# A home of their own for four sums of x, W' of A moved, W' ahead of the denominators, and a new order of TensorE's steps, in a gated mix of two linear-attention blocks

## The chip, the cores and the metric

One core of one Trainium2 chip runs the kernel. The metric is device time in microseconds (us). The kernel before takes 176.55 us, the median of three runs (176.12 to 176.67).

## The reference

Two linear-attention blocks, A and B, work on the same x (2,048 tokens by 640), and a sigmoid gate mixes their outputs. 32 heads have 20 columns each; phi(t) is t + 1 above 0 and exp(t) elsewhere, plus 1e-6.

```python
qkv = (x @ wqkv).reshape(B, S, 3, H, Dh) ...       # q, k, v by head
pq, pk = phi(q), phi(k)
kv = einsum("bhsd,bhse->bhde", pk, v);  z = einsum("bhsd->bhd", pk)
o = einsum("bhqd,bhde->bhqe", pq, kv) / (einsum("bhqd,bhd->bhq", pq, z) + 1e-6)
block = o.reshape(B, S, D) @ wo
out = g * A(x) + (1 - g) * B(x),   g = sigmoid((x * gate_w).sum(-1))
```

## The kernel before

Everything is bf16 with sums in fp32 PSUM (8 banks). The kernel never forms v: it multiplies pk's transpose by x (units G), then by wv (kv), then by wo, which gives one 640 by 640 matrix W' for each block; the output is scaled pq times W' of A plus scaled pq times W' of B. Products of 2 by 2 blocks are made with seven products in place of eight (a Strassen-Winograd scheme), which takes sums and differences of the operands on VectorE beforehand and combining steps on ScalarE and VectorE in between.

The stages, in order of time:

- Keys (0 to 48 us): x times wk for 16 tiles of 128 tokens, with phi on ScalarE and VectorE (L635 and L636 on TensorE).
- G and Q (48 to 106 us): five units G0 to G4 of seven steps, each step eight matmuls of 320 or 321 columns (L1029), woven together with five units Q0 to Q4 of seven steps, each two or three matmuls of 512 columns (L910). Q makes the queries of tokens 0 to 1,023 (blocks 0, 1). A step is named by its product, as in `G2.5` or `Q4.7`; a unit's steps come as 1, 2 and 5, 6, 3, 7, 4, and 6, 3, 7 and 4 add to a PSUM bank after a copy or combine. In G these are copies at L1058, combines at L1063 and sums z at L1077, and in Q copies at L965 and L919, combines at L924, and phi at L940 to L957.
- The middle (103 to 131 us): `kvA`, `kvB` (L1176), the denominators `dA0`, `dB0` (L1282, then VectorE L1304, ScalarE ln and exp, spread DMAs fx on SP, and the scaling of pq at L1349), the bursts of W' `wA0`, `wA1`, `wB0`, `wB1` (L1208, copied out at L1223 or L1225, stored to DRAM and loaded again in another layout by SP), and the queries of tokens 1,024 to 2,047: eight plain steps `R1A` to `R4B` (L997) and one seven-product unit `R0` (L910).
- Output (131 to 172 us): eight pairs of token tiles, O0 to O7, seven steps of five matmuls of 320 columns each (L1418), copies at L1434, L1457, L1462 and L1483, combines at L1441, and stores on SP.

The order of TensorE's steps is written out by hand in the string `MAIN` (L48). A planner in the kernel (`Sched`) takes it as it stands for TensorE, and orders the other engines' work by its own table of costs, due times and priorities; it also gives out PSUM banks. `TURN` is the planner's own charge for a change of the array's shape: full 128 by 128 (mode 0), denominators (1), W' (2), kv (3). `QD` and `RD` name the query tiles whose relu and add run as one VectorE instruction (L955, L1012); the others use ScalarE for the relu (L943, L1014) and VectorE for the add (L957, L1015).

SBUF is full, and buffers share space by age. `PKS` holds pk (columns 0 to 20,479, five units of 4,096) and behind it, from `SSB` = 20,480, the sums of pk, 3,072 columns for each unit. When G unit u has made its last product (`ulast[u]`), its part is free. Into these parts go, later, the sums of x for the seven-product query groups (`XU`, made by `x_sums` at L883: sums 1, 2, 4 at SSB, 5 and 3 elsewhere), the copies `SV`, W' of A (`WP["A"]`) and half of the output tiles (`ot`). Before the change the first group (Q, p = 0) and the second (R0, p = 1) use the same space for sums 1, 2 and 4, so that the second group's sums wait for all of Q's matmuls (`qpe[0]`); they are all made at token `X2` and wait for kvA too.

Of the kernel before, what the change touches and what calls it, by code (L numbers as in the profile page):

```python
# [11 lines left out]
D = 640  # L12
# [32 lines left out]
NPU = 5  # L45
SSB = 20480
RELUB = (3, 5, 7, 9, 11, 13)
MAIN = """G0.1 G1.1 G2.1 G1.2 G3.1 G2.2 G0.2 G1.5 G0.5 G1.6 G0.6 G1.3 G0.3 G2.5 G1.7 G2.6 G0.7 G2.3 G2.7 G0.4  # L48
G1.4 Q1.1 Q0.1 Q1.5 G2.4 Q0.2 Q0.5 Q0.6 G3.2 G3.5 Q0.3 G3.6 Q0.7 Q1.6 Q1.3 G3.3 Q2.5 G3.7 Q1.7 Q2.1
Q1.2 Q0.4 Q2.2 G3.4 Q2.6 Q3.1 Q4.1 Q4.5 Q2.3 Q1.4 Q3.2 Q4.6 Q2.7 G4.1 Q2.4 Q4.2 Q3.5 Q4.3 Q4.7 Q3.6  # L50
G4.2 G4.5 Q3.7 G4.6 Q4.4 Q3.3 Q3.4 G4.7 kvA X2 G4.3 G4.4 dA0 wA0 R1B wA1 LA dB0 S1 S0
kvB R2A wB0 R1A R3B R4A wB1 T1 R4B R0.1 R0.5 R2B R3A R0.2 R0.6 O0.1 O0.5 O3.1 O2.5 R0.7
R0.3 O0.2 O3.2 O2.1 O3.5 R0.4 O0.6 O3.6 O0.3 O3.3 O2.6 O2.2 O3.7 O1.1 dA1 dB1 S2 S3 O0.7 O2.3
O2.7 O1.2 O1.6 O0.4 O1.5 O1.7 O2.4 O4.1 O5.1 O7.1 O3.4 O1.4 O4.2 O5.2 O7.2 O5.5 O6.1 O5.6 O4.5 O6.2
O6.6 O5.7 O4.6 O5.3 O6.5 O7.6 O4.3 O4.7 O7.5 O7.7 O4.4 O7.3 O6.7 O5.4 O1.3 O6.3 O6.4 O7.4"""
RS = (0,)
PB = {}
PQH = (0,)
TP = {1: -0.5, 2: -1, 3: -0.4, 4: -0.3}
WPDVE = ("A1", "B0",)  # L60
QD = ("0.0A0", "0.1A0", "0.1B0", "0.2A0", "0.2B0", "0.3A0", "0.4B0", "0.4B1",)
RD = ("A1", "B0",)
LATE = {"ACT": 110.0, "DVE": 80.0}

# [32 lines left out]

HOP = 60.0  # L100
TURN = 100.0

class Sched:
# [16 lines left out]
    def run(self):  # L121
        todo = {e: [o for o in self.ops if o.eng == e] for e in self.ENGS}
        at = {e: 300.0 for e in self.ENGS}
        bus, mode = [0.0], 0
        live = {}
        left = {}
        for o in self.ops:
            for b in set(o.ins) | set(o.outs):
                if b.pool:
                    left[b] = left.get(b, 0) + 1  # L130

        def can(o, t):

            w = 0.0
            if o.behind is not None and o.behind.start is None:
                return None
            for d in o.deps:
                if d.end is None:
                    return None
                w = max(w, d.end + (0.0 if d.eng == o.eng == "PE" else HOP))  # L140
            skip = set()
            for b in o.outs:
                if b.pool and b.slot is None:
                    got = self.pick(b, max(w, t), skip)
                    if got is None:
                        return None
                    w = max(w, got[0]) if got[0] > t + 1e-6 else w
                    skip |= set(range(got[1], got[1] + b.n))
            return max(w, t) if o.eng == "PE" else w

        n = len(self.ops)
        while len(self.order) < n:
            best = None
            for e in self.ENGS:
                cand = todo[e]
                if not cand:
# [12 lines left out]
            if best is None:  # L169
                raise RuntimeError("stuck: " + ", ".join(c[0].name for c in todo.values() if c))  # L170
            (w, _, _), o, e = best
            for b in o.outs:
                if b.pool and b.slot is None:
                    self.take(b, w)
            for b in o.outs:
                o.deps += b.war
            w = max(w, at[e])
            if e == "PE" and o.mode != mode:
                w, mode = w + TURN, o.mode
            o.start = w  # L180
# [123 lines left out]
def body(nc, A_x, A_wqkv, A_wo, B_x, B_wqkv, B_wo, gate_w, out, log=None):  # L304
# [69 lines left out]
    PQ = {(X, 2 * p + h): PP[X, p][:, :, h, :] for X in XS for p in range(2) for h in range(2)}  # L374
    WVAf = WVA[:, :, :].rearrange("p c f -> p (c f)")
    WP, KVL = {}, {}
    for X, wp, kv in (("A", SSB + 6144, WVAf[:, 1920:2280]), ("B", 16384, PKS[:, 19584:19944])):
        WP[X] = PKS[:, wp : wp + NC * D].rearrange("p (g n) -> p g n", g=NC)
        KVL[X] = kv.rearrange("p (u f) -> p u f", u=NU)
    WST = {}  # L380
    for r, a in enumerate((GSAf[:, 0:1920], WVAf[:, 0:1920])):
        WST["A", r] = a.rearrange("p (u f) -> p u f", u=3)
        WST["B", r] = TXf[:, 1920 * r : 1920 * r + 1920].rearrange("p (u f) -> p u f", u=3)
    OST = {"os": [PKS[:, 8192 + D * k : 8832 + D * k] for k in range(NOS)], "ot": [PKS[:, SSB + D * k : SSB + D * k + D] for k in range(NOT)]}
    ZM = DEN[:, :].rearrange("p (i h) -> p i h", h=32)
    GGX = GSBf[:, 0:1024]
    GTX = EKT[:, 2576:3600]
# [482 lines left out]
    def x_sums(p, after):  # L870
        t1, t2 = 1024 * p, 1024 * p + 512
        a11, a12, a21, a22 = [XT[:, c : c + 2, lo : lo + 512] for lo in (t1, t2) for c in (0, 2)]
        for k, in0, in1, need in (
            (1, a21, a22, ()),
            (2, a11, XU[1], (1,)),
            (5, XT[:, 4, t1 : t1 + 512], XT[:, 4, t2 : t2 + 512], ()),
            (4, a12, XU[2], (2,)),
            (3, a21, a11, (1,)),
        ):
            bxu[p, k] = Buf("xu")  # L880
            op(
                "DVE",
                lambda e, out=XU.get((k, p), XU.get(k, a21)), in0=in0, in1=in1: e.tensor_tensor(out=out, in0=in0, in1=in1, op=ALU.subtract),  # L883
                dve2(512 if k == 5 else 1024),
                ins=[bxu[p, j] for j in need],
                outs=[bxu[p, k]],
                after=after,
                name="xu%d" % k,
            )

# [5 lines left out]
    def qu_unit(p, g):  # L896
# [33 lines left out]
        def post(X, h, pv, ins):  # L930
# [31 lines left out]
        def step(n):  # L962
# [297 lines left out]
    def wp_load(X, halves, lo, hi):  # L1260
# [316 lines left out]
```

## Time and profile before

| | |
|---|---|
| median of three runs | 176.55 us (176.12 to 176.67) |
| the profiled execution | 176.08 us, of which the span is 174.6 |
| TensorE busy | 171.1 us (98%), 1,320 matmuls recorded |
| its weight loads | 108.0 us, 1,335 |
| VectorE busy | 135.6 us (78%), 238 instructions |
| ScalarE busy | 114.2 us (65%), 218 instructions |
| granted TensorE clock | 1.0 |

A line such as L1029 is a line of the kernel; a row names engine, operation, output and inputs, shape and count. PE is TensorE's matmuls, PEld its weight loads, DVE VectorE, ACT ScalarE, SP the queue that issues most DMAs. The end of a matmul is modelled, so that rows of PE overlap; starts are better to go by. A few matmul records are missing in any trace; the weight loads are complete.

### The profile page before, as it was taken

The numbers are of one execution on the slowest core, as the hardware profiler recorded it, in microseconds if no ns is written. First come the engines' busy times: TensorE is split into PE (matmuls) and PEld (weight loads), VectorE is DVE, ScalarE is ACT, GpSimd is POOL, SyncE is SP. The second block draws the span as 40 slices with busy tenths as digits, with TensorE's granted clock in tenths as the row PEclk, the third lists the DMA queues.
The fourth block names the chain that finished last, engine by engine and source line by source line (L and its number), as shares of the span: only waits on it lengthen the run. The fifth ranks groups of instructions, "written<-read, shape, count | busy, mean of one in ns | idle before, by whom it ended". The sixth has DMA issues, their size and how long they took to land.

```text
span 174.6 us, 3344 instructions
## 1 busy us (share of the span) xinstructions
PE 171.1 (98%) x1320; PEld 108.0 (62%) x1335; DVE 135.6 (78%) x238; ACT 114.2 (65%) x218; POOL 5.1 (3%) x16
## 2 busy tenths in 40 slices
PE   9999999999999999999999999999999999999995
PEld 5555555555577767666655666655556667777773
DVE  2275996999999755846868879999999995898342
ACT  5378888988841221648699793867899865566332
POOL 2000000000000520000000000000000000000000
PEclk9999999999999999999999999999999999999999
DMA  6979999980000083554261001467670021450135
GB/s 198 295 142 195 190 374 364 350 158 6 4 0 0 0 71 82 99 130 101 41 184 41 0 4 39 97 187 185 243 188 18 0 75 33 92 192 0 38 122 179
DMA packets 33035, 20.59 MB, mean 118 GB/s; under 512 B 18260, under 2 KB 32892, under 8 KB 33020
## 3 DMA queue, kind: packets, MB, share of 16 engines
q1 hardware_dynamic: 32062, 19.76, 44.3%
q10 hardware_dynamic: 958, 0.63, 1.1%
q8 instruction: 10, 0.16, 0.4%
q14 instruction: 5, 0.04, 0.1%
HBM read 10.88 MB, written 4.26 MB: 87 GB/s over the span
## 4 chain that ended last, share of the span: by engine, by line
PE 90%; DVE 6%; ACT 2%; issue 1%; DVEq 0%
PE ps L1418 22%; PE ps L635 19%; PE ps L1029 19%; PE ps L910 12%; PE ps L997 9%; PE ps L636 6%; PE ps L562 1%; DVE WVA L1223 1%; ACT EQ L940 1%; DVE PKS L883 1%; PE ps L1282 1%; PE ps L1208 1%; PE ps L575 1%; DVE WKW L1063 1%; ACT PQ L943 1%
## 5 line engine op out<-in xcount | busy, mean ns | idle before, releaser
L635 PE MATMUL ps<-WKW,XT 128*128 128x512 bf16 x154 | 43.2, 382 | 0.0
L636 PE MATMUL ps<-WKW,XT 128*128 128x128 bf16 (+1 forms) x160 | 35.2, 220 | 0.3
L635 PEld LDWEIGHTS ps<-WKW,XT 128*128 128x128 bf16 x160 | 15.7, 98 | 19.1 <-DMA WKW<-in_A_wqkv_dram 0.3
L681 ACT ACTIVATE EKT<-ps 128x640 bf16<-128x640 f32 x32 | 22.4, 705 | 6.5 <-PE ps L636 5.8
L1029 PE MATMUL ps<-TX,PKS 128*128 128x321 bf16 (+1 forms) x160 | 23.8, 300 | 0.0
L1029 PEld LDWEIGHTS ps<-TX,PKS 128*128 128x128 bf16 x160 | 15.6, 98 | 7.2 <-DVE DEN L1077 0.3
L1029 PE MATMUL ps<-XN,PKS 128*128 128x321 bf16 (+1 forms) x120 | 17.7, 300 | 0.0
L1058 ACT ACTIVATE EKT<-ps 128x321 f32<-128x321 f32 (+1 forms) x15 | 6.4, 440 | 14.9 <-PE ps L1029 8.8
L636 PEld LDWEIGHTS ps<-WKW,XT 128*128 128x128 bf16 x160 | 15.8, 98 | 0.0
L1029 PEld LDWEIGHTS ps<-XN,PKS 128*128 128x128 bf16 x120 | 11.6, 98 | 5.2
L761 DVE TENSOR_TENSOR PKS<-PKS 128x1280 bf16<-128x1280 bf16 (+2 forms) x20 | 13.1, 686 | 0.1
L684 DVE TENSOR_SCALAR EKT<-EKT 128x1280 bf16<-128x1280 bf16 (+1 forms) x18 | 8.2, 454 | 5.9 <-ACT EKT L681 5.7
L940 ACT ACTIVATE EQ<-ps 128x512 bf16<-128x512 f32 x18 | 11.1, 614 | 2.1 <-DVE ps L924 1.4
L1063 DVE TENSOR_TENSOR WKW<-ps,EKT 128x320 bf16<-128x320 f32 x15 | 7.3, 490 | 6.4 <-PE ps L1029 5.8
L1008 ACT ACTIVATE EQ<-ps 128x1024 bf16<-128x1024 f32 x8 | 8.2, 1024 | 3.3 <-PE ps L997 2.6
L720 DVE SCALAR_TENSOR_TENSOR PKS<-ps,EKT 128x640 bf16<-128x640 f32 x12 | 9.9, 821 | 0.1
L910 PE MATMUL ps<-XT,WQA 128*128 128x512 bf16 x34 | 9.5, 379 | 0.1
L997 PE MATMUL ps<-XT,WQA 128*128 128x512 bf16 x37 | 9.0, 380 | 0.3 <-DVE PKS L1304 0.2
L997 PE MATMUL ps<-XT,WQB 128*128 128x512 bf16 x39 | 9.1, 380 | 0.2 <-issue 0.2
L693 ACT ACTIVATE PKS<-ps 128x640 bf16<-128x640 f32 x12 | 8.4, 698 | 0.0
L953 DVE TENSOR_SCALAR EQ<-EQ 128x512 bf16<-128x512 bf16 (+1 forms) x19 | 6.0, 322 | 2.7 <-ACT EQ L940 2.7
L1441 DVE TENSOR_TENSOR PKS<-ps,PKS 128x320 bf16<-128x320 f32 x8 | 3.9, 490 | 5.2 <-PE ps L1418 5.2
(155 smaller groups left out, 307.3 us busy)
## 6 DMA issues: line engine op xcount, KB each, us to landing
out_dram<-PKS SPq DMA_DIRECT2D x15, 160.0 KB, 1.8
XN<-in_A_x_dram SPq DMA_DIRECT2D x1, 2240.0 KB, 9.3
WKW<-in_A_wqkv_dram SPq DMA_DIRECT2D x5, 160.0 KB, 3.8
WKW<-in_B_wqkv_dram SPq DMA_DIRECT2D x5, 160.0 KB, 3.9
WQA<-in_A_wqkv_dram SPq DMA_DIRECT2D x1, 800.0 KB, 10.9
WQB<-in_B_wqkv_dram SPq DMA_DIRECT2D x1, 800.0 KB, 13.7
WVA<-in_A_wqkv_dram SPq DMA_DIRECT2D x1, 800.0 KB, 12.5
PKS<-in_B_wqkv_dram SPq DMA_DIRECT2D x1, 800.0 KB, 5.0
```

What stands on the lines that cost most here:

```text
L635: e.matmul(a[:, 0:512], l, WK[X][:, c, 0:512], start=(c == 0), stop=(c == NC - 1))
L636: return e.matmul(a[:, 512:w], l, WK[X][:, c, 512:w], start=(c == 0), stop=(c == NC - 1))
L681: op("ACT", lambda e, i=i, ps=ps: e.activation(evg(i), psg(ps), ACT.Exp), act_cost(D), ins=[ps] + first, outs=[ek, b], name="ke")
L693: op("ACT", lambda e, X=X, ps=ps: e.activation(pkt(X, t), psg(ps), ACT.Relu), act_cost(D), ins=[ps], outs=[rk], name="kr")
L720: lambda e, X=X, i=i, ps=ps: e.scalar_tensor_tensor(pkt(X, t), psg(ps), 0.0, evg(i), op0=ALU.max, op1=ALU.add),
L761: lambda e: e.tensor_tensor(out=out, in0=a, in1=b, op=ALU.subtract),
L910: r = e.matmul(PS[:, ps.slot, :], w, x, start=(first and i == 0), stop=(i == len(prs) - 1), skip_group_check=not first)
L940: o = [op("ACT", lambda e: e.activation(EQ[:, eq.slot + h, :], pv(), ACT.Exp), act_cost(512), ins=ins, outs=[eq], name="qe")]
L997: r = e.matmul(PS[:, ps.slot + h, :], WQ[X][:, c, g::5], XT[:, c, 1024 + 512 * h : 1536 + 512 * h], start=(c == 0), stop=(c == NC - 1))
L1029: r = e.matmul(PS[:, ps.slot, 0:w], reg[:, j, :], mov(j, w), start=(first and j == 0), stop=(j == 7), skip_group_check=not first)
L1063: lambda e: e.tensor_tensor(out=GT[:, dst.slot, lo : lo + HC], in0=PS[:, ps.slot, 0:HC], in1=PT[:, src.slot, 0:HC], op=ALU.add),
L1418: r = e.matmul(PS[:, ps.slot, 0:HALF], reg(g), mov(g), start=(first and g == 0), stop=(g == NC - 1), skip_group_check=not first)
```

## The change

1. The second group's sums 1, 2 and 4 of x get 3,072 columns of their own, at SSB + 6,144, the part of G unit 2. They now wait for `ulast[2]`, sum 5 for `ulast[1]`, and only sum 3 for kvA.
2. That space was W' of A's. It moves to SSB - 128, into the part of unit 0 (and the last 128 columns of pk), and its load waits for all of Q's matmuls and the last G unit in place of the fourth. The output tiles `ot` move from SSB to SSB + 3,072.
3. In `MAIN`, `wA0` comes ahead of `dA0`, and `kvB` ahead of `dB0`. The planner charges a turn from mode 1 to mode 2 with 190 instead of 100.
4. `MAIN` is laid out anew: the steps of G, Q, R0 and O stand in another order. The middle's sequence of R steps changes from R1A R3B R4A and R2B R3A at the end to R1A R4A R3B and R3A R2B.
5. `QD` names other tiles (two of the eight differ); `RD` names A0 as well. The plain relu of A (tokens 1,024 and on) waits for the scaling of blocks 0 and 1 only from step 2 on.

```diff
-MAIN = """G0.1 G1.1 G2.1 G1.2 G3.1 G2.2 G0.2 G1.5 G0.5 G1.6 G0.6 G1.3 G0.3 G2.5 G1.7 G2.6 G0.7 G2.3 G2.7 G0.4
-G1.4 Q1.1 Q0.1 Q1.5 G2.4 Q0.2 Q0.5 Q0.6 G3.2 G3.5 Q0.3 G3.6 Q0.7 Q1.6 Q1.3 G3.3 Q2.5 G3.7 Q1.7 Q2.1
-Q1.2 Q0.4 Q2.2 G3.4 Q2.6 Q3.1 Q4.1 Q4.5 Q2.3 Q1.4 Q3.2 Q4.6 Q2.7 G4.1 Q2.4 Q4.2 Q3.5 Q4.3 Q4.7 Q3.6
-G4.2 G4.5 Q3.7 G4.6 Q4.4 Q3.3 Q3.4 G4.7 kvA X2 G4.3 G4.4 dA0 wA0 R1B wA1 LA dB0 S1 S0
-kvB R2A wB0 R1A R3B R4A wB1 T1 R4B R0.1 R0.5 R2B R3A R0.2 R0.6 O0.1 O0.5 O3.1 O2.5 R0.7
...
-O6.6 O5.7 O4.6 O5.3 O6.5 O7.6 O4.3 O4.7 O7.5 O7.7 O4.4 O7.3 O6.7 O5.4 O1.3 O6.3 O6.4 O7.4"""
+MAIN = """G0.1 G1.1 G0.2 G3.1 G1.2 G0.5 G2.1 G0.6 G2.2 G1.5 G1.6 G0.3 G0.7 G1.3 G1.7 G3.5 G0.4 G2.5 G1.4 Q1.1
+G2.6 G3.6 G2.3 G2.7 Q1.5 G3.7 Q1.6 Q0.1 Q1.3 G2.4 Q1.7 Q4.1 Q1.2 G3.2 G3.3 Q0.5 Q0.6 Q0.2 Q2.5 G3.4
+Q0.3 Q1.4 Q0.7 Q2.1 Q4.5 Q0.4 Q3.1 Q4.6 Q4.2 Q2.6 Q2.3 Q4.3 Q2.2 Q4.7 Q3.6 Q3.2 Q4.4 G4.1 Q2.7 Q3.5
+Q3.7 G4.5 G4.2 G4.6 Q3.4 Q2.4 G4.7 Q3.3 kvA X2 G4.3 G4.4 wA0 dA0 R1B wA1 LA kvB dB0 S0
+R2A S1 wB0 R1A R4A R3B wB1 T1 R4B R3A R0.5 R0.1 R2B O0.1 R0.6 O2.5 O0.5 R0.2 R0.7 O3.1
...
+O6.6 O5.5 O4.5 O7.6 O6.7 O5.7 O4.3 O6.4 O5.3 O4.7 O6.3 O7.2 O7.5 O5.4 O7.7 O7.3 O4.4 O7.4"""
-QD = ("0.0A0", "0.1A0", "0.1B0", "0.2A0", "0.2B0", "0.3A0", "0.4B0", "0.4B1",)
-RD = ("A1", "B0",)
+QD = ("0.0A0", "0.1B0", "0.1B1", "0.2A0", "0.2B0", "0.2B1", "0.3A0", "0.4B0",)
+RD = ("A0", "A1", "B0",)
-TURN = 100.0
+TURN, TURNS = 100.0, {(1, 2): 190.0}
-                w, mode = w + TURN, o.mode
+                w, mode = w + TURNS.get((mode, o.mode), TURN), o.mode
-    for X, wp, kv in (("A", SSB + 6144, WVAf[:, 1920:2280]), ("B", 16384, PKS[:, 19584:19944])):
+    for X, wp, kv in (("A", SSB - 128, WVAf[:, 1920:2280]), ("B", 16384, PKS[:, 19584:19944])):
-    ... "ot": [PKS[:, SSB + D * k : SSB + D * k + D] for k in range(NOT)]}
+    ... "ot": [PKS[:, SSB + 3072 + D * k : SSB + 3712 + D * k] for k in range(NOT)]}
+    for k in (1, 2, 4):
+        XU[k, 0] = XU.pop(k)
+    for i, k in enumerate((1, 2, 4)):
+        XU[k, 1] = PKS[:, SSB + 6144 + 1024 * i : SSB + 7168 + 1024 * i].rearrange("p (c s) -> p c s", c=2)
-            after=[ulast[3]] if X == "A" else [],                       # load of W'
+            after=qpe[0] + [ulast[NPU - 1]] if X == "A" else [],
-            x_sums(1, qpe[0] + kva)
+            x_sums(1, lambda k: kva if k == 3 else [ulast[1 if k == 5 else 2]])
```

More of the change, by code (lines that the diff above doesn't have):

```diff
@@ L47 @@
 RELUB = (3, 5, 7, 9, 11, 13)
-MAIN = """G0.1 G1.1 G2.1 G1.2 G3.1 G2.2 G0.2 G1.5 G0.5 G1.6 G0.6 G1.3 G0.3 G2.5 G1.7 G2.6 G0.7 G2.3 G2.7 G0.4
-G1.4 Q1.1 Q0.1 Q1.5 G2.4 Q0.2 Q0.5 Q0.6 G3.2 G3.5 Q0.3 G3.6 Q0.7 Q1.6 Q1.3 G3.3 Q2.5 G3.7 Q1.7 Q2.1
-Q1.2 Q0.4 Q2.2 G3.4 Q2.6 Q3.1 Q4.1 Q4.5 Q2.3 Q1.4 Q3.2 Q4.6 Q2.7 G4.1 Q2.4 Q4.2 Q3.5 Q4.3 Q4.7 Q3.6
-G4.2 G4.5 Q3.7 G4.6 Q4.4 Q3.3 Q3.4 G4.7 kvA X2 G4.3 G4.4 dA0 wA0 R1B wA1 LA dB0 S1 S0
-kvB R2A wB0 R1A R3B R4A wB1 T1 R4B R0.1 R0.5 R2B R3A R0.2 R0.6 O0.1 O0.5 O3.1 O2.5 R0.7
-R0.3 O0.2 O3.2 O2.1 O3.5 R0.4 O0.6 O3.6 O0.3 O3.3 O2.6 O2.2 O3.7 O1.1 dA1 dB1 S2 S3 O0.7 O2.3
-O2.7 O1.2 O1.6 O0.4 O1.5 O1.7 O2.4 O4.1 O5.1 O7.1 O3.4 O1.4 O4.2 O5.2 O7.2 O5.5 O6.1 O5.6 O4.5 O6.2
-O6.6 O5.7 O4.6 O5.3 O6.5 O7.6 O4.3 O4.7 O7.5 O7.7 O4.4 O7.3 O6.7 O5.4 O1.3 O6.3 O6.4 O7.4"""
+MAIN = """G0.1 G1.1 G0.2 G3.1 G1.2 G0.5 G2.1 G0.6 G2.2 G1.5 G1.6 G0.3 G0.7 G1.3 G1.7 G3.5 G0.4 G2.5 G1.4 Q1.1
[3 more added lines that the diff above has]
+R2A S1 wB0 R1A R4A R3B wB1 T1 R4B R3A R0.5 R0.1 R2B O0.1 R0.6 O2.5 O0.5 R0.2 R0.7 O3.1
+R0.3 O0.2 O3.2 O3.5 R0.4 O2.1 O0.6 O0.3 O3.6 O3.3 O2.2 O2.6 O3.7 O1.1 dA1 dB1 S3 S2 O0.7 O1.2
+O2.7 O2.3 O0.4 O1.6 O1.5 O3.4 O1.7 O5.1 O4.1 O6.1 O2.4 O1.3 O1.4 O4.2 O6.2 O7.1 O5.2 O6.5 O5.6 O4.6
+O6.6 O5.5 O4.5 O7.6 O6.7 O5.7 O4.3 O6.4 O5.3 O4.7 O6.3 O7.2 O7.5 O5.4 O7.7 O7.3 O4.4 O7.4"""
 RS = (0,)
@@ L383, in body @@
         WST["B", r] = TXf[:, 1920 * r : 1920 * r + 1920].rearrange("p (u f) -> p u f", u=3)
-    OST = {"os": [PKS[:, 8192 + D * k : 8832 + D * k] for k in range(NOS)], "ot": [PKS[:, SSB + D * k : SSB + D * k + D] for k in range(NOT)]}
+    OST = {"os": [PKS[:, 8192 + D * k : 8832 + D * k] for k in range(NOS)], "ot": [PKS[:, SSB + 3072 + D * k : SSB + 3712 + D * k] for k in range(NOT)]}
     ZM = DEN[:, :].rearrange("p (i h) -> p i h", h=32)
@@ L874, in x_sums @@
             (1, a21, a22, ()),
-            (2, a11, XU[1], (1,)),
+            (2, a11, XU[1, p], (1,)),
             (5, XT[:, 4, t1 : t1 + 512], XT[:, 4, t2 : t2 + 512], ()),
-            (4, a12, XU[2], (2,)),
+            (4, a12, XU[2, p], (2,)),
             (3, a21, a11, (1,)),
@@ L882, in x_sums @@
                 "DVE",
-                lambda e, out=XU.get((k, p), XU.get(k, a21)), in0=in0, in1=in1: e.tensor_tensor(out=out, in0=in0, in1=in1, op=ALU.subtract),
+                lambda e, out=XU.get((k, p), a21), in0=in0, in1=in1: e.tensor_tensor(out=out, in0=in0, in1=in1, op=ALU.subtract),
                 dve2(512 if k == 5 else 1024),
@@ L886, in x_sums @@
                 outs=[bxu[p, k]],
-                after=after,
+                after=after(k),
                 name="xu%d" % k,
@@ L937, in post @@
             bpq[b, NC * XS.index(X) + g] = pqf
-            home = {("B", 0): lambda: [ulast[1]], ("A", 0): lambda: [], ("B", 1): lambda: list(qpe[0]), ("A", 1): lambda: qpe[0] + pqs_op["A", 0] + pqs_op["A", 1] + fx_op[2] + ([ulast[3]] if h else [])}[X, p]()
+            home = {("B", 0): lambda: [ulast[1]], ("A", 0): lambda: [], ("B", 1): lambda: list(qpe[0]), ("A", 1): lambda: qpe[0] + (pqs_op["A", 0] + pqs_op["A", 1] + fx_op[2] if g > 1 else []) + ([ulast[3]] if h else [])}[X, p]()
             one = ["%d.%d%s%d" % (p, g, X, i) in QD for i in range(2)]
@@ L969, in step @@
             elif n == 5:
-                mm(pz, True, [(WU[1][:, c, g::5], XU[1][:, c, :]) for c in range(2)] + [(wq("B", 4), xt(4, 1))], wqs + [bwu[1], bxu[p, 1]])
+                mm(pz, True, [(WU[1][:, c, g::5], XU[1, p][:, c, :]) for c in range(2)] + [(wq("B", 4), xt(4, 1))], wqs + [bwu[1], bxu[p, 1]])
                 d[5] = save(s5, pz)
             elif n == 6:
-                mm(px, False, [(WU[2][:, c, g::5], XU[2][:, c, :]) for c in range(2)], [bwu[2], bxu[p, 2]], [d[1]])
+                mm(px, False, [(WU[2][:, c, g::5], XU[2, p][:, c, :]) for c in range(2)], [bwu[2], bxu[p, 2]], [d[1]])
                 d[2] = save(s2, px)
             elif n == 3:
-                mm(pz, False, [(wq("B", 2 + c), XU[4][:, c, :]) for c in range(2)] + [(wq("B", 4), XU[5, p])], wqs + [bxu[p, 4], bxu[p, 5]], [d[5]])
+                mm(pz, False, [(wq("B", 2 + c), XU[4, p][:, c, :]) for c in range(2)] + [(wq("B", 4), XU[5, p])], wqs + [bxu[p, 4], bxu[p, 5]], [d[5]])
                 comb(pz, s2, False)
@@ L991, in qp_unit @@
         dst = PP[X, 1][:, g, :, :]
-        home = list(qpe[0]) + ([ulast[3]] + pqs_op["A", 0] + pqs_op["A", 1] + fx_op[2] if X == "A" else [])
+        home = list(qpe[0])
+        if X == "A":
+            home += [ulast[3]] + (pqs_op["A", 0] + pqs_op["A", 1] + fx_op[2] if g > 1 else [])
         def fn(e):
@@ L1499, in body @@
                     w_sums([ulast[0]])
-                    x_sums(0, [ulast[0]])
+                    x_sums(0, lambda k: [ulast[0]])
                     qsteps = [qu_unit(0, k) for k in range(NC)]
```

## The prediction

> **What bounds the kernel now.** First the page: busy times, then the span in slices and the chain that ended last.
>
> ```profile
> span 174.6 us, 3344 instructions
> ...
> PE 171.1 (98%) x1320; PEld 108.0 (62%) x1335; DVE 135.6 (78%) x238; ACT 114.2 (65%) x218; POOL 5.1 (3%) x16
> ...
> PE 90%; DVE 6%; ACT 2%; issue 1%; DVEq 0%
> ```
>
> TensorE (PE) is busy from its first matmul to its last, and the chain is TensorE itself. A gain must come from holes in its stream, or not at all. So next the waits, those of the weight loads (PEld), where a TensorE step waits:
>
> ```profile
> PEld ps L1208 <- issue: 1.1, 3, 0.4
> ...
> PEld ps L1418 <- ACT PKS L1462: 0.3, 2, 0.2
> ...
> PEld ps L1029 <- DVE DEN L1077: 0.3, 1, 0.3
> ```
>
> Away from the start and from changes of the array's shape ("issue", and L1208's and L1282's other rows) two name another engine: L1029 on VectorE's z sum (L1077), L1418 on ScalarE's copy (L1462). The timeline around the first:
>
> ```profile
> 61.80 0.26 DVE L1077 SCALAR_TENSOR_TENSOR DEN<-EKT,ps,CST 128x32 bf16<-128x32 f32 x1
> ...
> 62.11 1.48 PEld L1029 LDWEIGHTS ps<-TX,PKS 128*128 128x128 bf16 x12 [0.27 <-DVE DEN L1077]
> ```
>
> This is G2.5, which needs the PSUM bank of G1.3. G1.3, G0.3 and G2.5 signal their ends at 61.09, 62.19 and 63.39 in the trace: 1.09 for G0.3, 1.21 for G2.5, so the wait loses 0.12. It also gives my rule of thumb: the z sum ended at 62.05 and the stream went on at 63.39 - 1.09 = 62.30, so a release must come 0.25 ahead of a step's place. The second (136.42 and 137.10, O2.1 and O3.5) loses 0.02 by the same reckoning. All waits inside the run are worth 0.14.
>
> Then the shape changes, in the timeline from 106 to 113:
>
> ```profile
> 106.81 0.73 PE L1282 MATMUL ps<-PQ,DEN 128*32 128x256 bf16 x20
> ...
> 107.56 0.60 PE L1208 MATMUL ps<-WOA,WVA 64*60 64x320 bf16 x15
> ...
> 110.38 0.60 PE L1208 MATMUL ps<-WOA,WVA 64*60 64x320 bf16 x15
> ...
> 110.92 0.73 PE L1282 MATMUL ps<-PKS,DEN 128*32 128x256 bf16 x20
> ...
> 111.58 1.13 PE L1176 MATMUL ps<-GSB,PKS 128*64 128x60 bf16 x55
> ```
>
> From start to start, denominators (L1282) to W' (L1208) take 0.75, the same 20 matmuls to kv (L1176) 0.66, and W' to denominators 0.54. Only denominators-to-W' is longer, by 0.09.
>
> Last, busy time by stretch (columns: stretch, its length, PE, PEld, DVE, ACT, POOL, clock, DMA, GB/s):
>
> ```profile
> 83.00:104.00 21.00, 20.89 (x147) 12.70 (x147) 16.46 (x40) 18.18 (x38) 0.34 (x2) 1.00 0.21 55
> 104.00:118.00 14.00, 13.62 (x219) 8.57 (x216) 13.87 (x26) 8.81 (x14) 0.00 (x0) 1.00 0.43 105
> ```
>
> ScalarE has little air from 83 to 104, VectorE none from 104 to 118, yet TensorE hardly waits for either. The granted clock is 1.00 throughout.
>
> **The change, part by part.**
>
> *Matmuls.* Both programs hold 1,335 of them, of the same forms; RS is unchanged, and "A0" in RD names a unit that is not built that way. Cost 0.
>
> *Sums of x in their own home.* Three sums of 0.69 (L883) no longer wait for kv of A, nor the 0.42 one; only sum 3 does. Some 2.5 us of VectorE leave the full stretch 104 to 118 for the time after G2.4 and before 83, where VectorE is under two thirds busy (7.39 of 12 us from 71 to 83). Nothing on TensorE waited for them: the first step of the second seven-product group runs at 124.6, the last sum ended at 113.35. Gain 0. They can hurt only by standing in front of a combine (below).
>
> *W' of A in another place.* Its load (SP, 120.44) now waits for the first seven-product group and G4.4 instead of G3.4; both are over before 107 in either order. The second OUT store pool moves with it and still waits for both query groups. Cost 0.
>
> *W' ahead of denominators, kv of B ahead of the second.* Before, the shapes run: full, denominators, W', full, W', denominators, kv, full. After: full, W', denominators, full, W', kv, denominators, full. Seven changes each; the 0.75 one is gone. Denominators to full I price by the later pair, 1.21 for 40 matmuls on the chain at 144.04, so 0.66 for 20: no excess. W' to kv and kv to denominators do not occur; the nearest rows are W' to denominators (0.54, no excess) and kv to full (1.05, the same at both kv). The one excess seen is 0.09, so bounds are -0.09 and +0.09 on top; I take 0, since of the nine kinds in the trace only that one shows an excess of more than 0.03. Term: -0.09, bounds -0.18 to +0.09. The Trainium skill, page "TensorEngine Tiling (Array Packing)", section Tiling Modes (Key Properties), says that changing the tiling mode drains TensorE, whichever mode; counted so, seven against seven gives 0 and the sum below would be 0.09 less of a gain. The rows differ by kind, and no run here yet shows the new kinds.
>
> What moves behind it: the first denominators start 0.54 later. On ScalarE a W' copy (0.97) now stands ahead of ln and exp, on VectorE a 1.15 copy ahead of L1304; then four spread DMAs on SP, in unchanged order (gs, fx, wps, wpl). VectorE reaches L1304 about 0.55 later (108.07 before), and SP's first spread DMA starts no more than that later (109.89); the scaling of PQ that waits for it (114.32 to 126.06) feeds TensorE from O0.1 on, at 131.05. Behind these on the queues stand only such steps. Cost 0; without that cover 0.55. kv of B comes about 0.75 earlier after G4.4. It needs the DMA transpose of the last block:
>
> ```profile
> 106.42 0.49 DVE L1063 TENSOR_TENSOR WKW<-ps,EKT 128x320 bf16<-128x320 f32 x1
> ...
> 106.94 2.52 SPq L429 DMA_TRANSPOSE GSB<-WKW  x2
> ```
>
> The pair landed at 110.83, and kv's loads began at 111.58, so 0.75 of cover would go entirely. But the combine at 106.42 stood behind the first late sum of x (105.72, 0.69), G4.3 having signalled at 105.81; with that sum gone the transposes start up to 0.5 earlier. Cost 0, bound +0.2.
>
> *The new order.* G2.5 no longer follows G0.3: -0.12 (bounds -0.12 and 0). O0.2, O3.2, O3.5 keep their distance: 0.02 stays. New narrow places, each against the 0.25:
> - Q2.5 takes the bank that G3.3's z sum frees, with eight 512-column matmuls (8 x 0.216 = 1.73) between. Chain: release 0.02, a running instruction on VectorE 0.18, combine 0.49, a query combine of 0.69 that stands between, z sum 0.26, less two overlaps of 0.085, plus 0.25: 1.72. Cover 0.01. Such a chain cost 0.12 at G2.5; I take +0.05, bounds 0 and +0.7 (one more 0.69 in front).
> - Q0.4 and Q4.4 follow Q0.7 and Q4.7 by 1.08. Before, Q2.4 followed Q2.7 by 1.09 with the combine ending at 92.99, G4.1's signal at 93.36 and Q2.4's 0.65 later for 3 x 0.216: no loss, 0.12 of cover. Cost 0.
> - Q3.6, Q4.7 and Q3.5 wait at 92 to 96 for copies in a ScalarE run without a gap. At 0.51 from start to start they have 0.04 to 0.1; in the trace such copies (614 mean) start 0.48 to 0.52 apart. Cost 0, bounds 0 and +0.5.
>
> *End.* The last step is O7.4 in both, then a 0.44 copy and a store of 1.6; the stores ahead of it are 0.33 of SP each and 0.6 apart. 0.
>
> **Sum:** -0.09 - 0.12 + 0.05 = -0.16. The profiled execution took 176.08 (span 174.6 and 1.5 around it); the median is 176.55, 0.47 above it. So 176.4 by the median, a profiled one near 175.9. About 0.3%, 0.53 us, is what a measurement of this kernel can tell from no change; this is a third of that.
>
> **Rivals.**
> 1. *ScalarE becomes the bound between 84 and 98 (slower).* For: 18.18 of 21 us busy, and the new order asks for 12 us of it without a pause. Against: the 0.48 spacing. It decides when one further 0.5 instruction stands ahead of a copy at Q3.6, Q4.7 or Q3.5, whose covers are under 0.1: 0.4 each, and as the steps hang on one another, two of them: 0.8 - 0.16 = +0.64, 177.2. Chance 0.11.
> 2. *The home does not pay and nothing else does:* the stalls move (Q2.5 takes the loss of G2.5, a new shape change that of the old). 0: 176.55. Chance 0.25, within the bound.
> 3. *kv of B meets its transposes:* 0.2 lost instead of 0.16 won, 176.6. Chance 0.07, within.
> 4. *Every hole closes:* all of 0.14 and 0.09 with 0.09 more at the new changes, 176.2. Only with the scatter of the runs (176.12 to 176.67) would that show as over 0.3%. Chance 0.12, of which 0.08 beyond the bound.
>
> My forecast, a gain under the bound, holds 0.45. Within 0.3% then is 0.45 + 0.25 + 0.07 + 0.04 = 0.81; faster 0.08; slower 0.11. The range: 176.55 - 0.32 and 0.15 of scatter for the low end, 176.05; at the high end rival 3 with scatter and half of rival 1's price, 176.85.
>
> **What would show it.** Right: no L1077 wait of TensorE near 62; L1208 to L1282 at 0.54 and no step of 0.75; L1176 to L1282 at 1.05; the last matmul 0.1 to 0.2 earlier. Wrong: TensorE waits for L965, L919 or L924 between 81 and 98, a wait of L1176 for a DMA near 110.8, or a last matmul later than before.

## The result, and the profile after

| | before | after |
|---|---|---|
| median of 14 runs each, side by side | 176.34 us (176.02 to 177.02) | 176.90 us (176.43 to 177.64) |
| ratio, 95% interval | | 1.0032 (1.0018 to 1.0046) |
| the profiled execution, its span | 176.08, 174.6 | 176.75, 175.3 |
| end signal of the last key product to end signal of the last product of O7.4 | 124.54 | 125.08 |

The changed kernel is slower by 0.56 us, where 0.16 less was forecast; it lies just above the high end of the range. A second series gave 1.0029 (1.0014 to 1.0044). The last row leaves out the first 48 us, whose input loads scatter by several tenths from run to run: the stretch that the change touches grew by 0.54.

The page of the changed kernel:

```profile
span 175.3 us, 3351 instructions
...
PE 172.2 (98%) x1335; PEld 108.2 (62%) x1335; DVE 135.4 (77%) x236; ACT 114.4 (65%) x218; POOL 4.5 (3%) x16
...
PE 96%; DMA 2%; ACT 0%; issue 0%; DVE 0%
```

The chain that ended last is still TensorE's, but 2% of it is now a DMA, and none was there before. The waits of TensorE name it (matmuls first, then weight loads; the columns are the sum, the number and the longest wait):

```profile
PE ps L1182 <- DMA GSB<-WKW: 0.7, 1, 0.7
...
PEld ps L1182 <- issue: 1.3, 2, 0.9
...
PEld ps L1003 <- DVE EQ L957: 0.2, 1, 0.2
...
PEld ps L1424 <- ACT PKS L1468: 0.2, 1, 0.2
```

L1182 is kv (L1176 before). The wait for the z sum at G2.5 is gone, that for the output copy (L1468) is left. The timeline around kv of B:

```profile
106.17 0.49 DVE L1069 TENSOR_TENSOR WKW<-ps,EKT 128x320 bf16<-128x320 f32 x1
...
106.69 2.52 SPq L433 DMA_TRANSPOSE GSB<-WKW  x2
...
106.86 0.60 PE L1214 MATMUL ps<-WOA,WVA 64*60 64x320 bf16 x15
...
107.40 0.73 PE L1288 MATMUL ps<-PQ,DEN 128*32 128x256 bf16 x20
...
110.34 0.60 PE L1214 MATMUL ps<-WOA,WVA 64*60 64x320 bf16 x15
...
111.59 1.06 PEld L1182 LDWEIGHTS ps<-GSB,PKS 128*64 128x64 bf16 x55 [0.89 <-issue]
111.62 1.13 PE L1182 MATMUL ps<-GSB,PKS 128*64 128x60 bf16 x55 [0.67 <-DMA GSB<-WKW]
...
112.68 0.73 PE L1288 MATMUL ps<-PKS,DEN 128*32 128x256 bf16 x20
```

W' to denominators takes 0.54 (106.86 to 107.40), kv to denominators 1.06: as forecast, no shape change costs more than its matmuls, and the 0.75 of before is gone. But from the first matmul of W' to the first weight load of kv it takes 1.25 (110.34 to 111.59), where the same pair takes 0.53 in a run shown below (e2) in which nothing is late. kv of B stood still for 0.7 us.

It waited for the second of the two DMA transposes issued from 106.69, called gsB4 here (the first is gsB3). gsB3 was issued at 106.69 and landed 2.57 later. gsB4 was issued at 107.94 and landed at 111.48, 3.55 later; in the kernel before, 2.63 later. So the combine and the transposes did start 0.25 earlier (106.17 and 106.69 against 106.42 and 106.94), and the landing was 0.66 later all the same. The DMA view of just these 3.55 us (packets, MB, share of 16 engines; then KB and us from issue to landing):

```profile
q1 hardware_dynamic: 1318, 0.32, 46.0%
q14 instruction: 1, 0.01, 0.5%
...
GSB<-WKW SPq DMA_TRANSPOSE x1, 3.5
```

One packet is not data: 8 KB of instructions for one of the engines, at 109.91, 0.31 us long. In the kernel before the packet of its kind came at 105.74, ahead of both transposes. The same view of gsB4 there, from 108.19 to 110.83, has as many packets of data:

```profile
q1 hardware_dynamic: 1318, 0.32, 61.2%
...
GSB<-WKW SPq DMA_TRANSPOSE x1, 2.6
```

So it was not more data on the DMA engines that made the landing late.

Two measures are used from here on. A step's cover is the time by which what it needs is done ahead of its place in TensorE's order. A step's loss is the distance of its end signal from that of the step before, less what the same matmuls take where nothing is waited for. By it the kernel before loses 0.11 at G2.5 and 0.02 at O3.5, and 0.09 at its denominators-to-W' pair. The changed kernel loses 0.75 at kv of B and 0.02 at O3.5, nothing else. 0.75 - 0.11 - 0.09 = +0.55: the 0.54 of the table, and the 0.56 of the medians.

### The profile page after: what moved, and what is told of

It reads as the page before. It is cut to its first block, busy times and chain, and to the rows that moved or that the text cites. A ratio compares the mean times of both kernels' runs of the same rounds, so it can differ in the third digit from the quotient of the medians.

```text
span 175.3 us, 3351 instructions
## 1 busy us (share of the span) xinstructions
PE 172.2 (98%) x1335; PEld 108.2 (62%) x1335; DVE 135.4 (77%) x236; ACT 114.4 (65%) x218; POOL 4.5 (3%) x16
## 4 chain that ended last, share of the span: by engine, by line
PE 96%; DMA 2%; ACT 0%; issue 0%; DVE 0%
PE ps L1035 22%; PE ps L1424 22%; PE ps L639 20%; PE ps L914 13%; PE ps L1003 9%; PE ps L640 5%; DMA GSB<-WKW 2%; PE ps L566 1%; PE ps L1182 1%; PE ps L1288 1%; PE ps L1214 1%; PE ps L579 1%; ACT PKS L1489 0%; ACT GSA L1231 0%; DVE ONE L465 0%
## 5 line engine op out<-in xcount | busy, mean ns | idle before, releaser
L639 PE MATMUL ps<-WKW,XT 128*128 128x512 bf16 x160 | 44.4, 383 | 0.0
L914 PE MATMUL ps<-XT,WQA 128*128 128x512 bf16 x36 | 10.4, 379 | 0.0
L1003 PE MATMUL ps<-XT,WQA 128*128 128x512 bf16 x40 | 9.2, 381 | 0.0
L923 ACT ACTIVATE PKS<-ps 128x512 f32<-128x512 f32 x12 | 7.4, 624 | 1.6 <-PE ps L914 1.6
```

What stands on the lines that cost most here:

```text
L639: e.matmul(a[:, 0:512], l, WK[X][:, c, 0:512], start=(c == 0), stop=(c == NC - 1))
L914: r = e.matmul(PS[:, ps.slot, :], w, x, start=(first and i == 0), stop=(i == len(prs) - 1), skip_group_check=not first)
L1003: r = e.matmul(PS[:, ps.slot + h, :], WQ[X][:, c, g::5], XT[:, c, 1024 + 512 * h : 1536 + 512 * h], start=(c == 0), stop=(c == NC - 1))
```

## The experiments

The theories, by the letters of the texts below. A: kv of B's cover was moved away, and the transpose landed late because an instruction packet came into it. B: the transpose is late by the place it has in the new order, the packet is chance. C: the position of kv of B costs by itself. A2: behind the wait at kv of B there is a second one at R0.6, and with both gone the forecast 0.16 is there. D and E stand beside it.

The main runs, with the stretch from the last key product to the last product, the 8 KB packet nearest the transposes, gsB4's time from issue to landing, and the losses. A ratio is to the kernel before on the same chip; a dash is a run timed once. The other eight runs, which tried to move the packet, stand under "Packet or place?".

| run | ratio (95%) | stretch | packet at | gsB4 | loss at kv of B | at R0.6 |
|---|---|---|---|---|---|---|
| before | 1 | 124.54 | 105.74 | 2.63 | 0 | 0 |
| changed | 1.0032 (1.0018 to 1.0046) | 125.08 | 109.91, inside | 3.55 | 0.75 | 0 |
| e6, changed again | 1.0029 (1.0014 to 1.0044) | 125.14 | 109.86, inside | 3.62 | 0.82 | 0 |
| e1 | 0.9996 (0.9983 to 1.0008) | 124.72 | 109.64, inside | 3.51 | 0.05 | 0.34 |
| e2 | 1.0012 (0.9997 to 1.0027) | 124.48 | 105.73 | 2.64 | 0.01 | 0.15 |
| e3 | 0.9993 (0.9978 to 1.0009) | 124.59 | 106.37 | 2.64 | 0.06 | 0 |
| e4 | 1.0005 (0.9991 to 1.0018) | 124.60 | 98.48, 105.84 | 2.64 | 0.07 | 0 |
| e5 | 0.9978 (0.9962 to 0.9994) | 124.49 | 110.27, inside | 3.58 | 0.12 | 0 |
| e9 | 0.9987 (0.9968 to 1.0006) | 124.37 | 105.42 | 2.64 | 0.01 | 0 |
| e10 | 0.9983 (0.9968 to 0.9999) | 124.33 | 105.60 | 2.64 | 0.01 | 0 |
| e12 | 1.0024 (1.0011 to 1.0037) | 125.15 | 109.75, inside | 3.59 | 0.79 | 0 |
| e11 | - | 125.03 | 110.04, inside | 3.50 | 0.70 | 0 |

### Is it kv of B, and is it its place? (e1 to e4)

**e1**, the denominators ahead of kv of B again:

```diff
-... R1B wA1 LA kvB dB0 S0
+... R1B wA1 LA dB0 S0 kvB
```

> The changed kernel with one pair exchanged back: the denominators of B stand ahead of kv of B again, as before the change. Theory A (kv of B reaches its place before the last DMA transpose of gs of B has landed, because the denominators no longer stand between, and that transpose takes 3.55 us instead of 2.6): the transpose may land as late as in the changed kernel, but kv of B comes 0.66 to 0.75 later in the order, so it waits 0 to 0.1 instead of 0.75. 176.15 to 176.35 us where the changed kernel has 176.90, and in the trace no loss over 0.1 at kv of B. Rival C (the new order of the whole section costs it, and the wait only shows there): 176.8 to 177.0, with the 0.75 showing at another step. The rival that the later transpose is the new order's traffic says the same as A here.

The transpose landed as late as ever (3.51) and cost 0.05, since the denominators' 0.66 stood in between. kv of B is the place. But the stretch is 124.72, where the forecast 0.16 would give 124.38: 0.34 was lost at a step no one had named, R0.6, of which more below.

**e2**, the changed kernel with VectorE's program made eight instructions longer at its very start:

```diff
+    DUM = sb("DUM", [128, 32], bf)
+    for i in range(8):
+        op("DVE", lambda e, i=i: e.memset(DUM[:, i : i + 1], 0.0), 60.0, name="dum")
```

> The changed kernel with eight small memsets added to VectorE's program at its very start, where it is idle; everything else, the order included, is the same. That shifts VectorE's instruction fetches to some 5 to 7 us earlier work. Theory A with an instruction fetch as the cause (the 8 KB packet at 109.91 us that lies inside the transpose of gsB4): the packet leaves 107.9 to 110.5, the transpose lands 2.6 us after its issue at about 110.55, kv of B waits 0 to 0.05, 176.05 to 176.3 us: about 0.75 below the changed kernel and 0.1 to 0.25 below the kernel before. Rival B (the transpose is late by the new order's own transfers or by its place, and the packet only happens to lie there): the landing stays near 111.4, 176.8 to 177.0. If the packet is another engine's, it stays at 109.9 and so does the time, and nothing is told.

The packet moved to 105.73, so it is VectorE's. With it gone the DMA view of gsB4 and the timeline of the same place read

```profile
q1 hardware_dynamic: 1315, 0.32, 60.9%
...
GSB<-WKW SPq DMA_TRANSPOSE x1, 2.6
```

```profile
110.78 0.60 PE L1217 MATMUL ps<-WOA,WVA 64*60 64x320 bf16 x15
...
111.31 1.03 PEld L1185 LDWEIGHTS ps<-GSB,PKS 128*64 128x64 bf16 x55 [0.18 <-issue]
...
112.37 0.45 PEld L1291 LDWEIGHTS ps<-PKS,DEN 128*32 128x32 bf16 x20
```

(three lines further down in the code). W' to kv takes 0.53. Order, transfers and places are those of the changed kernel, and kv of B lost 0.01. That speaks against B. The time, 1.0012 (0.9997 to 1.0027), is above what was expected, and its interval reaches into that of the changed kernel; the trace is what decides here. Its stretch is 0.6 shorter than the changed kernel's, and only 0.06 below that of the kernel before, since 0.15 was lost at R0.6.

**e3**, the kernel before with kv of B ahead and nothing else of the change:

```diff
-... LA dB0 S1 S0
-kvB R2A wB0 ...
+... LA kvB dB0 S1 S0
+R2A wB0 ...
```

> The kernel before with one pair exchanged: kv of B ahead of the denominators of B and the two selections, as the change puts it, and nothing else of the change. Theory A: the transposes there take 2.57 and 2.63 us and the last lands at about 110.83; kv of B's place is then about 111.0 and its release is needed 0.25 ahead, so it waits 0 to 0.1: 176.2 to 176.45, no different from before. Rival C (the position alone costs, with no late transpose): 0.66 to 0.75 lost, 177.0 to 177.1.

0.9993, 0.06 lost: C falls. Without a late transpose the cover of 0.75 was all spare, but then only just: 0.06 was already missing.

**e4**, e3 with thirty copies on ScalarE to bring its packet into the transpose:

```diff
+    DUM = sb("DUM", [128, 32], bf)
+    for i in range(30):
+        op("ACT", lambda e, i=i: e.activation(DUM[:, i : i + 1], EPSC[:, :], ACT.Copy), 200.0, after=pk_last[-1:], prio=10**7, name="dum")
```

> The run before this one (the kernel before with kv of B ahead of the denominators) with thirty one-column copies added to ScalarE at about 52 to 56 us, where it is idle. That brings ScalarE's instruction fetch, at about 131.8 us in the kernel before, forward to some 109 to 110 us, into the last DMA transpose. Theory A with the fetch as cause: if the 8 KB packet falls between 107.9 and 110.5, the transpose lands 0.5 to 1.0 later, kv of B waits 0.5 to 1.0, 176.8 to 177.3. If the packet falls outside, as without the copies: 176.2 to 176.45. Rival B (a fetch does not matter): 176.2 to 176.45 wherever it falls.

The packet went to 98.5, too far. Nothing is told, but that the copies cost nothing.

### The second hole, R0.6 (e5, e9, e10, e12)

In the middle the change put R3A ahead of R0.5, R0.1 and R2B. e1 shows what that did. ScalarE (ACT, and ACTq for the DMAs that it issues) and the weight loads of R0.6 in e1:

```profile
124.23 1.86 ACTq L433 DMA_DIRECT2D wpsB<-TX  x2
126.14 1.02 ACT L1014 ACTIVATE EQ<-ps 128x1024 bf16<-128x1024 f32 x1 [1.33 <-DVE PKS L1355]
...
129.77 0.63 ACT L923 ACTIVATE PKS<-ps 128x512 f32<-128x512 f32 x1
130.25 0.65 ACT L969 ACTIVATE ps<-ps 128x512 f32<-128x512 f32 x1
...
130.94 0.16 PEld L914 LDWEIGHTS ps<-PKS,WKW 128*128 128x128 bf16 x2 [0.47 <-ACT ps L969]
```

R0.6 adds to a bank that ScalarE must first copy (L923, L969, at 129.77 and 130.25). Ahead of those copies stand four evacuations (copies out of PSUM) of R4B and R3A, and ahead of these ScalarE issues two stores of W' of B itself, 1.86 us long here and 0.93 in the kernel before. The same places there:

```profile
124.70 0.93 ACTq L429 DMA_DIRECT2D wpsB<-TX  x2
...
128.02 0.60 ACT L919 ACTIVATE PKS<-ps 128x512 f32<-128x512 f32 x1
...
130.62 0.33 PEld L910 LDWEIGHTS ps<-PKS,WKW 128*128 128x128 bf16 x2
```

In e1 R4B had signalled at 124.75; its evacuation started at 126.14. The view puts that wait down to a VectorE sum that had ended at 125.60; the issue ended at 126.09.

**e5** is e1 with the four steps as they stood before the change:

```diff
-R2A S1 wB0 R1A R4A R3B wB1 T1 R4B R3A R0.5 R0.1 R2B O0.1 R0.6 O2.5 O0.5 R0.2 ...
+R2A S1 wB0 R1A R4A R3B wB1 T1 R4B R0.5 R0.1 R2B R3A R0.6 O0.1 O2.5 O0.5 R0.2 ...
```

> The run with the denominators of B ahead of kv of B again, with one more stretch put back as it stood before the change: R0.5, R0.1, R2B, R3A, R0.6 instead of R3A, R0.5, R0.1, R2B, O0.1, R0.6. In the run without this, R0.6 at 130.94 us waited 0.34 for ScalarE's second copy of the query products ahead of it (done 130.89), because ScalarE had two evacuations of R3A ahead of it and had stood 0.86 us behind two stores of W' that it issues itself. Theory A2 (behind the wait at kv of B the new order hides a second one, at R0.6, and the 0.2 that the prediction forecast is there once both are gone): no wait at R0.6, the last product ends 0.3 earlier than in that run, 176.0 to 176.2 us, 0.15 to 0.4 below the kernel before. Rival D (there is no gain to be had: the forecast 0.2 was never there, or ScalarE is late elsewhere): 176.35 to 176.5, with the 0.3 back at another step within 10 us.

No wait at R0.6, and the last product 0.23 earlier than in e1. By its times, 0.9978 (0.9962 to 0.9994), this version is 0.4 us below the kernel before, and below the changed one, which had 1.0029 (e6) in the same series. The stretch shows only 0.05 of these 0.4, since 0.12 is still lost at kv of B; where the rest would come from was not found. D falls as far as it said that the 0.3 would come back at another step: it did not.

**e9** closes both holes the other way: kv of B ahead as changed, e2's memsets, e5's order.

> The changed kernel, its kv of B ahead of the denominators as changed, with the eight memsets on VectorE (so that the instruction packet comes before the last transpose) and R0.5, R0.1, R2B, R3A, R0.6 in the order of before. Theory A2: neither wait is left (kv of B 0 to 0.05, R0.6 none), all products end 0.1 to 0.3 earlier than in the kernel before, 0.15 to 0.45 less time: a ratio of 0.9975 to 0.9990. Rival C (kv of B's place itself is wrong): 0.1 to 0.7 above the run that had the denominators first (0.9978).

The stretch is 124.37, 0.17 under the kernel before: the forecast 0.16, with 0.02 lost at O3.5 and 0.04 at O2.1. The ratio of 0.9987 agrees and does not by itself tell it from 1, nor from e5.

**e10** asks which part of ScalarE's lateness it is: e2, the order as changed, with all stores of W' on SP.

```diff
-                    "ACT" if X == "B" and r == 0 else "SP",
+                    "SP",
```

> The run with the eight memsets alone (R0.6 waited 0.15 there for ScalarE's copy), with the four stores of W' of B that ScalarE issues given to SP. Theory A2, second part (ScalarE is late at R0.6 because it stands 1.3 us behind its own two stores at 125 us): its evacuation of R4B starts 0.6 to 0.8 earlier, the wait at R0.6 is gone, 0.15 less than that run: ratio 0.998 to 1.000 to the kernel before. Rival E (it is the order of ScalarE's evacuations, two of R3A ahead, whatever the stores do): 0.1 or more of the wait stays.

ScalarE's evacuation of R4B starts 0.02 after R4B's signal (124.99), where e1 took 1.39, and the copy that R0.6 needs ended at 130.15, 0.7 ahead of the step:

```profile
125.01 1.02 ACT L1017 ACTIVATE EQ<-ps 128x1024 bf16<-128x1024 f32 x1
...
129.53 0.62 ACT L972 ACTIVATE ps<-ps 128x512 f32<-128x512 f32 x1
...
130.88 0.59 PE L917 MATMUL ps<-PKS,WKW 128*128 128x512 bf16 x2
```

0.9983 (0.9968 to 0.9999), and a stretch of 124.33, the shortest of all. The two evacuations of R3A still stand ahead of the copies. So either suffices: the order of before with ScalarE's stores (e5, e9), or the order as changed without them. The order alone doesn't make the wait; E falls.

**e12**, the changed kernel with e5's order only:

> The changed kernel with R0.5, R0.1, R2B, R3A, R0.6 in the order of before and nothing else: the packet and kv of B's wait stay. Theory A2: the wait at R0.6 lay hidden behind the 0.75 at kv of B, so this brings 0 to 0.05: ratio 1.0025 to 1.0045 to the kernel before, kv of B waits 0.7 to 0.85. Rival (R0.6 cost the changed kernel something by itself): 0.15 to 0.35 less.

1.0024, 0.79 lost at kv of B: closing the second hole alone brings nothing that can be measured, since TensorE comes 0.75 late to R0.6 anyway. In the changed kernel the copy ended at 131.23, R0.6 started at 131.43.

### Packet or place? (e6 to e8, e11 and the last six)

**e6** is the changed kernel again.

> The changed kernel once more, unchanged, beside the others on one chip. Theory A: the 8 KB instruction packet lies in the last transpose again (it comes at a fixed point of VectorE's program, with its 185th instruction), so the landing takes 3.4 to 3.6 us, kv of B waits 0.65 to 0.8, and the time is 176.7 to 177.0. If the packet's place were chance: no wait, and 176.3 to 176.7.

It repeats to 0.1: packet at 109.86, landing 3.62, loss 0.82.

**e7** and **e8**, e4 with 22 and 20 copies:

> The kernel before with kv of B ahead of the denominators, and 22 small copies on ScalarE instead of 30: with 30 ScalarE's 8 KB fetch came at 98.5 us, with none at 132.1, so with 22 it should come at about 106 to 110. Theory A: if it falls between 107.9 and 110.5, the last transpose (2.64 us in the runs with 30 and with none) lands 0.5 to 1.0 later and kv of B, whose release was 0.06 late there, waits 0.5 to 1.0: 176.8 to 177.4. Outside of that stretch, or by rival B (a fetch does not matter): 2.64 and 176.3 to 176.6.

> As the run before, with 20 copies: the fetch a little later, at about 108 to 113 us. Theory A: between 107.9 and 110.5 the transpose lands 0.5 to 1.0 later; later than 110.9 it changes nothing there (2.64).

The packet came at 120.4 and 121.9, behind the transpose, which took 2.64 and 2.63; kv of B lost 0.05 and 0.06, e7 is 0.9989 (0.9975 to 1.0004). (R3A lost 0.23 in e7. The trace puts that down to ScalarE: its two stores took 1.54 us there, and R3A's loads waited for an evacuation behind them, L1017. With 28 copies, below, the stores took 1.58 and R3A lost 0.27; where they took 0.93 to 1.25, in the kernel before and in this order, it lost nothing.)

**e11**, the changed kernel with four memsets in place of eight:

> The changed kernel with four memsets on VectorE at the start where eight were added before. The packet came with VectorE's 184th to 185th instruction both times, so now at about 107.4 to 108.0: inside the transpose of gsB3 (issued 106.7, landing 2.57 later without a packet), mostly before that of gsB4. Theory A: gsB3 lands 3.3 to 3.6 after its issue, gsB4 2.6 to 2.7, and kv of B waits 0 to 0.1, since gsB3 at about 110.2 is still the earlier. Rival B (the last transpose is late by its own place): gsB3 2.57, gsB4 3.5, and 0.75 lost.

My idea of where the packet lies was wrong. It did not move (110.04), and gsB4 was late (3.50). The numbers are those that B was given, but as the packet lay in gsB4 again, the run doesn't tell the two apart. What it does tell: memsets as such do not take the delay away. With four of them the packet stays inside and the loss is 0.70, with eight it is outside and the loss is 0.01.

Six more runs tried to place the packet. Four of them, with 25 to 28 copies on ScalarE in e3's order:

> The kernel before with kv of B ahead of the denominators, and 25 small copies on ScalarE at 52 to 56 us. ScalarE's 8 KB packet came at 132.1 us with none, 121.9 with 20, 120.4 with 22 and 98.5 with 30, in steps that no simple count explains; between 22 and 30 it should cross the last transpose (108 to 110.5). Theory A: in the run where it lies there, and only there, gsB4 lands 3.4 to 3.7 us after its issue instead of 2.64 and kv of B loses 0.7 to 1.0 instead of 0.06. Rival B: 2.64 and 0.06 wherever the packet lies.

> As with 25 copies, with 26: by a straight line between 22 and 30 the packet would come at about 109 to 111. Theory A: in the window, gsB4 3.4 to 3.7 and 0.7 to 1.0 lost at kv of B; outside, 2.64 and 0.06. Rival B: 2.64 and 0.06 in either case.

> As with 25 copies, with 27: packet at about 106 to 110. Theory A and rival B as there.

> As with 25 copies, with 28: packet at about 103 to 108, likely ahead of the last transpose. Theory A: 2.64 and 0.06 then; if it lies behind 108, as in the window. Rival B as there.

ScalarE's packet jumped from 120.4 (22 copies) to 103.1 (25), and came at 102.1, 102.2 and 101.5 with 26, 27 and 28: it never fell between. gsB4 took 2.63 to 2.64 in all four and kv of B lost 0.05 to 0.06. The last two, five and six memsets on VectorE in the changed kernel:

> The changed kernel with five memsets on VectorE at the start. With four its 8 KB packet came at 110.0 us (with the 189th instruction, inside the transpose of gsB4), with eight at 105.7 (with the 184th). If the packet moves to the 184th here, it comes at about 106.5 to 107.5, inside the transpose of gsB3 (issued 106.7 to 107.0): by theory A gsB3 then lands 3.3 to 3.6 after its issue instead of 2.57, gsB4 2.6 to 2.7, and kv of B waits 0 to 0.1. If it stays near 110: gsB4 3.5 to 3.6 and 0.7 to 0.8 lost. By rival B gsB3 lands at 2.57 in either case.

> As with five memsets, with six. With the 184th instruction the packet would come at about 106 to 107, at the edge of the transpose of gsB3: theory A gives gsB3 2.57 to 3.5 by how much of it lies inside, gsB4 2.64, no wait at kv of B. If it stays near 110: gsB4 3.5 to 3.6 and 0.7 to 0.8 lost.

The packet stayed at 109.98 and 110.28, gsB4 took 3.50 and 3.63, kv of B lost 0.71 and 0.84.

Together: eight traces of the new order have the packet inside gsB4, and it took 3.50 to 3.63 in all; twelve traces, of both orders, do not, and it took 2.63 to 2.64 in all. In the new order the packet was taken away by memsets, and the delay went with it. The transfers themselves bear the packet's mark: in the eight, 9 to 16 of gsB4's 640 data packets start late, up to 2.51 to 2.69 us after the issue; in the twelve all have started by 2.16. This no longer fits B, by which the packet only happens to lie there.

The loss needs both halves. With the packet inside but the denominators in between it is 0.05 to 0.12 (e1, e5); with the cover gone but no packet inside, 0.01 to 0.07 (e2, e3, e4, e7 to e10 and the runs with 25 to 28 copies); with both, 0.70 to 0.84. That the packet, planted into the order of the kernel before, would do the same is not shown: no run could place it there.

## Why the prediction was wrong

**kv of B, the step that failed.** The prediction saw that the change takes 0.75 of cover from this step, set against it that the transposes start up to 0.5 earlier, and wrote "Cost 0, bound +0.2". They started 0.25 earlier. The failure is the other half: it took the 2.6 us from issue to landing for a constant, and let the bound rest on that. The last landing took 3.55. The rival *kv of B meets its transposes* named the meeting, though not the late landing; its price of 0.2 measured 0.75, and its chance was 0.07. With 0.75 there, the sum would have read 0.75 - 0.09 - 0.12 + 0.05 = +0.59, against the 0.54 of the stretch.

That landings vary stood in the trace of before. Most transposes of WKW took 2.57 to 2.64 there, but two did not. The one issued at 64.32 took 3.94; an instruction packet of 16 KB had started at 64.16. The one issued at 88.12, again into GSB, took 4.88 with no instruction packet in it, shortly after a load of weights issued at 87.53. The DMA views from 64 to 68.26 and from 88.12 to 93.01:

```profile
q1 hardware_dynamic: 1728, 0.43, 95.1%
q8 instruction: 1, 0.02, 2.4%
...
GSA<-WKW SPq DMA_TRANSPOSE x1, 3.9
```

```profile
q1 hardware_dynamic: 1328, 0.98, 73.7%
...
GSB<-WKW SPq DMA_TRANSPOSE x1, 4.9
```

In the first another transpose was in flight too, and in the window of the second three times the data of gsB4's was moved, 0.98 MB against 0.32, so neither is a clean case. As a bound for a late landing they were to be had, 1.3 and 2.3 above the usual one. And e3's 0.06 says that the cover left was below zero even without a packet.

**The narrow places: one was missing.** R0.6 is not in the list. With R3A moved ahead of R0.5 its cover fell from 2.0 us (copy done at 128.62, weight loads from 130.62, in the kernel before) to 0.2 in the changed kernel (131.23 and 131.43). Where the wait at kv of B is gone, it loses 0.15 to 0.34 (e2, e1), which is the whole of the forecast gain. In the changed kernel it costs nothing, so it is not why the result is what it is; it is why e2 and e1 only come back to the kernel before.

**The rest of the sum held.** G2.5: 0.12 forecast, 0.11 measured, gone in every run with the new order. The shape changes: 0.09 forecast; W' to denominators 0.54, W' to kv 0.53, kv to denominators 1.06, all without excess. The rule of the Trainium skill that the prediction weighed (page "TensorEngine Tiling (Array Packing)", Tiling Modes), that a change of mode drains TensorE, counted alike for all modes, gives 0 for seven changes against seven. The rows show a price by pair instead: 0.09 for denominators to W', and no excess for the pairs that took its place. Q2.5: +0.05 forecast, no loss, within its bounds. The first denominators moved back by 0.54 at no cost. VectorE's load from 104 to 118 fell, by 1.7 of the 2.5 foreseen, and ScalarE's from 83 to 104 rose, without a loss at Q3.6, Q4.7 or Q3.5, so the main rival on the slower side did not come:

```profile
83.00:104.00 21.00, 21.00 (x144) 12.50 (x143) 16.39 (x38) 19.27 (x40) 0.25 (x2) 1.00 0.41 78
104.00:118.00 14.00, 13.33 (x222) 8.21 (x217) 12.13 (x22) 8.88 (x14) 0.00 (x0) 1.00 0.40 95
```

(Columns as in the prediction; ScalarE, the fourth, 18.18 before and 19.27 now; VectorE, the third, 13.87 and 12.13 in the second stretch.) With both holes closed, e9's stretch is 0.17 shorter against the 0.16 of the sum.

One sum in the prediction does not come out: the high end of the range, rival 3 with scatter and half of rival 1's price, is 176.6 + 0.15 + 0.32 = 177.07, not 176.85.

So the direction was wrong by one term out of four, and the chances were wrong in the same place: a step that loses all its cover had been given 7 in 100.

## What to carry to other kernels

When a change takes the cover away between a DMA and the step that needs it, do not price the landing by the usual one alone: look up the slow landings of its kind in the trace and what ran beside each. That can be data, and it can be the program's own instruction packets, which an edit far ahead can move (eight memsets did here, four to six did not). When a hole of 0.7 opens, look for the next step behind it that has become tight; closing the first shows only what the second leaves. And ScalarE stood still here while it issued its two stores, for 0.84 to 1.86 us, which no busy time shows; work behind such an issue needs cover for it.

## What the runs showed of the hardware

- The profile counts instruction packets on the same 16 DMA engines as data (q14, 8 KB, two of which followed edits of VectorE's and ScalarE's programs; q8, 16 KB). One 8 KB packet of 0.31 to 0.39 us goes with 0.9 to 1.0 us more for a 2.6 us transpose. The Trainium skill, page "Runtime: NRT & Kernel Launch", section Instruction fetch mechanics, says that an engine's sequencer fetches the next page over a DMA queue of its own, in blocks of 16 KiB, and that the cost of crossing a boundary is mostly hidden. The rows agree in that the packets stand apart from the data's queue (q1), though VectorE's and ScalarE's both stand under q14; the size doesn't agree (VectorE's packet has 8 KB). VectorE lost nothing by it (it waited for W' until 110.99 anyway), but a transfer of another queue paid, and TensorE 0.75 behind it.
- Less than half of the delay is in the data. In the changed kernel 12 of gsB4's 640 data packets start late, and the last of its small closing packets 0.38 us later after the issue than in the kernel before. From there to the first of the 16 semaphore increments that tell of the landing it takes 0.88 us, against 0.32 where no packet came; all 16 then come within 0.12. Why the increments come so late is open.
- Where the packet comes is no plain count of instructions: four to six memsets at the start of VectorE's program left it at 110.0 to 110.3, eight moved it by 4.2 us.
- The same two stores issued by ScalarE held its queue for 0.93, 1.28 and 1.86 us (before, changed, e1). Why the time varies was not tested.
